# A planned two-branch kernel (S4D convolution and Hedgehog attention): Abs as an operation of its own, new planned durations, new order

## The chip, the cores and the metric

The kernel runs on one core of one Trainium2 chip. The metric is the device time of one execution in microseconds. The engines are TensorE (PE; its weight loads are listed as PEld), VectorE (DVE), ScalarE (ACT), GpSimd (POOL) and SyncE (SP), whose queue issues every transfer of this kernel. L12 is line 12 of the kernel before.

## The reference, cut to what matters

Two branches that do not depend on each other share the output, 576 columns each, for 2048 positions.

```python
# A: S4D. K is made from 576 x 128 modes, then a causal convolution along 2048 positions.
P = exp((A * dt[:, None])[:, :, None] * pos)          # A = -exp(log_A_real) + 1j * A_imag
K = 2.0 * einsum("dn,dnl->dl", C, P).real
y = irfft(rfft(u_t, 2 * L) * rfft(K, 2 * L))[..., :L] + u * D_skip
# B: linear attention, 32 heads of 18, with a learned feature map
q, k, v = split(x @ wqkv)                             # 576 -> 3 x 576
phi_q = concat(softmax(q @ w_phi), softmax(-q @ w_phi))   # phi_k likewise
o = phi_q @ (phi_k.T @ v) / (phi_q @ sum(phi_k) + 1e-6)
b = o @ wo
out = concat(a, b)
```

## The kernel before, in words

Branch B. The feature weights are folded into the weights of k and q (`fold`, L472 to L488): five blocks of wkT, each times w_phi on TensorE, then split on ScalarE and VectorE into a high and a low part, wh and wl. The weights of v (and later of the output) are loaded in thirds and split the same way (`whole`, L503 and L504). Sixteen key tiles of 128 positions follow: the tile of x is loaded, split into xh and xl (L512, L436), and multiplied in three products (`gemm`, 378, 378 and 396 columns wide). Each is three times as many matmuls as its size, since high and low parts are multiplied apart. Then come the two softmaxes (`softmax`, L547 to L559) and a product into kvt, which all sixteen tiles add to. Sixteen query tiles do the same with 2 x 288 columns, turn the features with TensorE (L646), multiply them with kv, divide, turn again (L676) and multiply with the output weights.

Branch A. The Fourier transforms are products with small matrices. `u_first` makes the first step for u (16 blocks). The 36 groups make the convolution kernel K: GpSimd adds phases as whole numbers (`phases`, L853 to L858) in cs[:, 1], a tile of 128 x 1040; `waves` (L868 to L870) turns them into a cosine and a sine on ScalarE, three instructions in one operation of the plan: the absolute value of the phases into cs[:, 0], the sine of the phases, the sine of (pi/2 minus the absolute value). `group` multiplies out the exponents on TensorE (L422, `ps<-sel,mg`), takes Exp on ScalarE (L891), multiplies them on VectorE with the waves (L897 to L902, into cs and E) and sums over the modes on TensorE (`ps<-E,cs`). After each 9 groups `k_first` transforms that quarter. Sixteen products and sixteen last steps follow (`product`, `last`), the products half by half of the columns; each product loads its parts from DRAM and writes back there.

What sets the order. Nothing runs in the order of the text. Each operation is recorded with its engine, a planned duration, and the buffers that it reads and writes (`op`). `run` then plays the kernel through with a clock for each engine, takes again and again the operation that can start first (with ties by a due time), and emits its instructions. A due time is the WANT of the unit (a key tile, a group, a product) minus the LEAD of its step. Some operations have two engines to choose from (`copy` with "any": ScalarE or VectorE; `tt` with two engines: GpSimd or VectorE), and `run` gives them to the engine on which they end first, with LEAN_ACT or LEAN_POOL as a handicap. Where the play has TensorE idle before a new PSUM buffer is written, `emit` puts products of zeros there (L213, fillers), whose result is overwritten, so that TensorE stays busy. The play takes TensorE at half rate for a window when it was little used in the window before. A transfer is played as 625 ns of SP, a start at 1300 ns, a duration by `c_dma`, and LAG until others see it; a change of the shape in which TensorE's array is used (`mode`) costs it extra. Planned durations go into the order alone: the chip does not know them.

The lines that the change touches are the LAG table (L166), the costs in `run` (L319 to L334), `c_dma` (L366), the tables of STAY, LEAN, LEAD and WANT (L372 to L401), the planned cost of `gemm` (L530), `waves` (L864 to L872) and the planned cost of the exponents in `group` (L889).

Of the kernel before, what the change touches and what calls it, by code (L numbers as in the profile page):

```python
# [11 lines left out]
I32 = mybir.dt.int32  # L12
AF = mybir.ActivationFunctionType
# [144 lines left out]
class Plan:  # L158
# [4 lines left out]

    LAG = dict(pe=200.0, dve=135.0, act=150.0, pool=110.0, sp=100.0)  # L166

    def __init__(self):
        self.ops, self.pools, self.free, self.window, self.strict = [], {}, {}, {}, {}
# [46 lines left out]
    def run(self):  # L216
# [48 lines left out]
        while done < n:  # L265
# [50 lines left out]
            self.engine[k] = e  # L316
            self.emit(k, o, e, nf)
            self.start[k] = s
            cost = 625.0 if e == "sp" else o[1] if e == o[0] else o[12][1]  # L319
            if e == "pe":  # L320
                while win < s // WINDOW:
                    warm = used >= (0.375 if warm else 0.7) * WINDOW
                    win, used = win + 1, 0.0
                extra = 50.0 if o[10] == mode else 95.0 + o[10][1] / 1.2
                mode = o[10]
                cost *= 1 if warm else 2
                used += cost * o[7]
                cost += extra if warm else 2 * extra
# [44 lines left out]
LEAD = dict(g1=510.8480, g2=65.9825, g3=1186.0588, g4=-101.5925, k1=55.5339, k2=-7.9693, k3=78.1520, k4=-179.0201, l1=-298.6070, p1=496.9566, p2=-165.1848, p3=26.4674, p4=392.3588, q1=25.7015, q2=-3.5201, q3=-402.9704, q4=-159.0330, q5=-59.1678, q6=-965.4445, u1=1381.3374)  # L373
FILL = 222.0


WANT = dict(
    ident=[-39.703],
    fold=[-3814.5703, -4514.447, 174.1103, 544.6624],
    start=[726.2842],  # L380
    key=[-2909.7917, -0.0799, 220.563, 157.8162, -225.5153, 173.04, -1241.6879, -109.3988, -338.4576, -175.3779,
          -2318.8196, 176.0873, 249.8555, 251.9596, -231.4053, 99.8816],
    kv=[85.5267],
    query=[476.857, 1690.9897, 4431.7125, 751.3041, 2777.2337, 589.8585, 3194.9953, 2789.5574, 367.711, 1380.6418,
          914.5124, 1423.5053, 2499.5972, 1377.3193, 2733.1361, 817.2673],
    u=[-102.8226, -226.0234, -1433.3706, -445.0721, -485.8874, -1597.2828, 880.8324, -734.4783, 728.5016, 739.4667,
          -177.0395, 249.377, -557.77, 773.8434, 166.2647, -5869.6701],
    mags=[-2640.9703],
    sel=[-2760.3264, -489.0097],
    dsk=[46.8315],  # L390
    par=[-3778.6822, 2.4322, 9.7494, 463.2853, 408.4987, 743.2542],
    group=[-219.8582, -466.9395, -327.3681, -1227.057, -1108.9783, -1278.4472, -63.1016, -322.7369, -865.4363, 67.264,
          -45.5422, 473.8194, 485.4349, 462.8623, 544.4259, 128.5531, 59.2296, -27.0576, 750.8126, 602.241, 749.2426,
          752.9731, 692.4676, 603.6052, 928.9227, 702.8443, 689.0661, 1091.0495, 1745.4579, 1177.32, 1030.5714,
          1356.2207, 1245.0883, 1029.2843, 1226.1579, 1186.6316],
    kfirst=[-2069.12, -388.4536, -152.51, 676.399],
    product=[580.2793, 583.4571, 524.945, 1019.1475, 645.2543, 381.769, 375.2706, 687.6813, 2038.1628, 2418.0025,
          2088.0002, 1103.4417, 2475.9162, 1427.038, 1252.1902, 1625.8165],
    last=[326.0515, 549.9183, 360.8347, 614.2391, 1189.7141, 171.5588, 558.2575, -103.0095, 1111.1706, 1441.7724,
          1346.2631, 1230.7698, 2479.1252, 3727.1339, 1655.5831, 3612.5906],  # L400
)  # L401


def body(tc, nc, i, out, ctx):
# [113 lines left out]
    def gemm(x, w, done, ps, o, cs):  # L518

        (xh, xl), (wh, wl) = x, w  # L520

        def f():
            p = o()
            for k in range(4):
                mm(p, xh.t[:, k, :], wh.t[:, k, cs], k == 0, False)
                mm(p, xh.t[:, k, :], wl.t[:, k, cs], False, False)
                mm(p, xl.t[:, k, :], wh.t[:, k, cs], False, False)
            mm(p, xh.t[:, 4, :], wh.t[:, 4, cs], False, False)
            mm(p, xh.t[:, 4, :], wl.t[:, 4, cs], False, True)
        op("pe", 14 * max(110, (cs.stop - cs.start) / 2.4 + 11.5), f, r=[xh, xl, *done], w=[ps], with_=[wh, wl], busy=0.93)  # L530

    def gemm_halves(x, w, done, c0):
        r = []
# [330 lines left out]
    def waves(cs):  # L864
        pl.step("g1")

        def f():
            act.activation(cs.t[:, 0], cs.t[:, 1].bitcast(I32), AF.Abs)  # L868
            act.activation(cs.t[:, 1], cs.t[:, 1].bitcast(I32), AF.Sin, scale=TURN)  # L869
            act.activation(cs.t[:, 0], cs.t[:, 0], AF.Sin, scale=-TURN, bias=hp.t)  # L870
        op("act", 3 * c_act(65 * W) + 370, f, r=[cs, hp], w=[cs], table="sin")
        return cs  # L872

    def group(g, par, cs, ks):
# [7 lines left out]
        def size(k, n):  # L882
            ps = [B("ps", [128, W, 32]) for _ in range(n)]

            def f():
                for h in range(n):
                    hs = slice(64 * h, 64 * h + 64)
                    mm(ps[h].t.rearrange("p x y -> p (x y)"), mg.t[hs, gi, :], sel.t[hs, k:k + 512])
            op("pe", 233, f, r=[mg, sel, cs], w=ps, with_=[E], mode=(64, 128))  # L889
            for p in ps:  # L890
                op("act", c_act(512), lambda p=p: act.activation(p.t, p.t, AF.Exp), r=[p], w=[p], table="exp")  # L891
            return ps
# [186 lines left out]
```

## Time and profile before

| | before |
|---|---|
| time, median of 3 runs | 623.44 us (620.82 to 626.74) |
| the profiled execution, its own time | 622.21 us |
| its span | 620.4 us |
| mean granted clock of TensorE | 0.979 |
| instructions in the profile | 19048 |

The page gives one execution. Its first part is the busy time of each engine, with the share of the span and the number of instructions. A row of a group is line, engine, operation, output from input, shapes and count; then the busy time and the mean length of one; then the engine's idle time ahead of them, and who ended it. A row of a window is its start and end, its length, then busy time and count for each engine (PE, PEld, DVE, ACT, POOL, or for the instructions of one line alone), the granted clock of TensorE, the share of the transfer engines and GB/s. A row of a timeline is start, length, engine, line, operation and count. A row of waits is who waited, for whom, the total, the number of times and the longest.

### The profile page before, as it was taken

To read this page: it belongs to the slowest core of one execution; us is meant where nothing else is said; L and a number is where in the kernel's file an instruction comes from. 1 tells how busy PE (TensorE), PEld (TensorE's weight loads), DVE (VectorE), ACT (ScalarE), POOL (GpSimd) and SP (SyncE) were. 2 spreads that over 40 slices of the span, in tenths; PEclk is the share of its full clock that TensorE was granted. 3 is DMA by queue.
4 is the path that set the end of the run, shared out by engine and by line. 5 is a ranking of instruction groups with operands and counts; after the bars stand their busy time and mean duration, and the time that the engine had idled before them with its cause. 6 is when DMAs were issued, how large, how long until landed. Compare 5 with 4: busy or idle time off the path is not lost.

```text
span 620.4 us, 19048 instructions
## 1 busy us (share of the span) xinstructions
PE 588.6 (95%) x7734; PEld 462.5 (75%) x7737; DVE 557.9 (90%) x1269; ACT 401.1 (65%) x605; POOL 269.1 (43%) x438
## 2 busy tenths in 40 slices
PE   8997999999999987998899999999999999999996
PEld 4687998999998765876666776668778867677775
DVE  3998999999999998999999999999998779987773
ACT  3868749889775399859687988898844322432120
POOL 0465356868451456255275685473301043233000
PEclk9997999999999998997999998999999999999999
DMA  8757110111123665655847668856563787876476
GB/s 230 223 206 234 46 43 23 45 51 50 45 65 99 157 209 203 214 178 151 238 137 237 193 197 227 230 169 211 161 192 88 194 278 220 244 222 220 156 225 195
DMA packets 97789, 104.01 MB, mean 168 GB/s; under 512 B 10534, under 2 KB 84134, under 8 KB 97702
## 3 DMA queue, kind: packets, MB, share of 16 engines
q1 hardware_dynamic: 97702, 102.80, 55.6%
q8 instruction: 61, 1.00, 0.7%
q14 instruction: 26, 0.21, 0.1%
HBM read 63.63 MB, written 39.06 MB: 166 GB/s over the span
## 4 chain that ended last, share of the span: by engine, by line
PE 59%; DVE 21%; ACT 9%; DMA 6%; issue 3%; SPq 1%; DVEq 0%; ACTq 0%
PE ps L422 55%; DVE ac L440 3%; PE ps L646 2%; DVE E L898 2%; DVE cs L897 2%; DVE total L557 2%; DMA dt<-in_ldt_dram 2%; DMA dram<-zi 1%; ACT cs L870 1%; ACT cs L868 1%; DVE E L902 1%; ACT cs L869 1%; DVE E L900 1%; PE ps L213 1%; ACT ps L891 1%
## 5 line engine op out<-in xcount | busy, mean ns | idle before, releaser
L422 PE MATMUL ps<-wh,xl 128*128 128x288 f32 (+2 forms) x448 | 141.5, 316 | 0.6 <-DVE xl L436 0.5
L422 PE MATMUL ps<-wh,xh 128*128 128x378 f32 (+2 forms) x400 | 134.6, 337 | 1.4 <-ACT zi L427 0.6
L422 PE MATMUL ps<-wl,xh 128*128 128x378 f32 (+2 forms) x400 | 129.3, 324 | 0.7 <-DVE wl L488 0.7
L858 POOL TENSOR_TENSOR cs<-cs,pi 128x512 int32<-128x512 int32 (+4 forms) x180 | 115.2, 644 | 10.1
L422 PEld LDWEIGHTS ps<-wh,xh 128*128 128x128 f32 x400 | 76.4, 191 | 14.0 <-issue 4.1
L422 PEld LDWEIGHTS ps<-wh,xl 128*128 128x128 f32 x448 | 85.1, 190 | 1.1 <-DVE xl L436 1.1
L422 PEld LDWEIGHTS ps<-wl,xh 128*128 128x128 f32 x400 | 76.5, 191 | 1.0 <-DVE wl L488 1.0
L891 ACT ACTIVATE ps<-ps 128x512 f32<-128x512 f32 x108 | 56.5, 580 | 9.3 <-PE ps L422 9.0
L436 POOL TENSOR_TENSOR ac<-ac 128x288 f32<-128x288 f32 x55 | 43.3, 808 | 41.8 <-DVE ac L440 32.3
L436 POOL TENSOR_TENSOR xl<-xi,xh 128x512 fp32r<-128x512 f32 x22 | 31.2, 1417 | 64.1 <-PE ps L422 30.1
L213 PE MATMUL ps<-zero 128*32 128x256 bf16 (+11 forms) x270 | 51.5, 327 | 3.2 <-DVE zero L456 1.2
L555 ACT ACTIVATE e<-e 128x1152 f32<-128x1152 f32 x32 | 37.4, 1169 | 22.8 <-DVE e L436 17.9
L440 DVE TENSOR_TENSOR ac<-us,ps 128x288 f32<-128x288 f32 x128 | 48.6, 444 | 1.7 <-issue 0.9
L422 PE MATMUL ps<-E,cs 128*32 128x64 f32 x2304 | 42.7, 224 | 7.2 <-DVE E L900 4.6
L422 PEld LDWEIGHTS ps<-E,cs 128*32 128x32 f32 x2304 | 35.2, 111 | 18.5 <-DVE E L900 7.1
L422 PE MATMUL ps<-wh,xi 128*128 128x288 f32 x160 | 48.9, 308 | 0.0
L512 ACT ACTIVATE xh<-xi 128x640 fp32r<-128x640 f32 x32 | 23.6, 738 | 36.5 <-DMA xi<-in_xT_dram 23.7
L422 PE MATMUL ps<-wl,xi 128*128 128x288 f32 x160 | 46.9, 295 | 0.0
L897 DVE TENSOR_TENSOR cs<-ps,cs 128x1024 f32<-128x1024 f32 x36 | 43.7, 1214 | 3.5 <-ACT ps L891 3.3
L422 PEld LDWEIGHTS ps<-kvb,fT 126*128 126x128 f32 (+1 forms) x320 | 38.2, 189 | 8.5 <-issue 2.1
L213 PEld LDWEIGHTS <-zero 128*128 128x128 bf16 (+6 forms) x273 | 25.9, 103 | 23.8 <-issue 12.1
L898 DVE TENSOR_TENSOR E<-ps,cs 128x1024 f32<-128x1024 f32 x36 | 43.6, 1210 | 0.1
(145 smaller groups left out, 1340.5 us busy)
## 6 DMA issues: line engine op xcount, KB each, us to landing
xi<-in_xT_dram SPq DMA_DIRECT2D x32, 320.0 KB
dram<-zi SPq DMA_DIRECT2D x16, 576.0 KB
dram<-zi SPq DMA_DIRECT2D x32, 288.0 KB
ub<-dram SPq DMA_DIRECT2D x32, 288.0 KB
kb<-dram SPq DMA_DIRECT2D x32, 288.0 KB
dram<-zo SPq DMA_DIRECT2D x32, 288.0 KB
zi<-dram SPq DMA_DIRECT2D x16, 576.0 KB
ub<-in_u_dram SPq DMA_DIRECT2D x16, 288.0 KB
```

What stands on the lines that cost most here:

```text
L213: self.matmul(t[0:cols, 0:n], self.zero.t[0:rows, 0:cols], self.zero.t[0:rows, 0:n])
L422: pe.matmul(o, l, r, start=start, stop=stop, skip_group_check=skip)
L436: op(eng, [c_dve(n) if e == "dve" else c_pool(n) for e in eng], lambda e: (dve if e == "dve" else pool).tensor_tensor(dst(), a(), b(), op= ...
L440: op(eng, c_dve(n) if eng == "dve" else c_pool(n), lambda: e.tensor_tensor(dst(), a(), b(), op=alu), r=r, w=w, lock=eng == "pool" or not a ...
L512: op("act", c_act(640) + 40, lambda: act.activation(xh.t, xi.t, AF.Copy), r=[xi], w=[xh])
L555: op("act", c_act(1152) + 40, lambda: act.activation(e.t, e.t, AF.Exp), r=[e], w=[e], table="exp")
L557: op("dve", 1270, lambda: dve.tensor_reduce(sm.t.rearrange("p h s -> p s h"), e.t, axis=AX.X, op=ALU.add), r=[e], w=[sm])
L646: pe.transpose(tp.t[0:m, j - j0, :], e.t[:, sign, 7 * g:7 * g + GRP[g], :].rearrange("p h f -> p (h f)"), ident.t)
L858: op("pool", c_pool(2 * n * W), lambda n=n, j=j: pool.tensor_tensor(x()[:, :, :, n:2 * n], x()[:, :, :, 0:n], pi.t[:, j:j + 2, gs].bitcast ...
L891: op("act", c_act(512), lambda p=p: act.activation(p.t, p.t, AF.Exp), r=[p], w=[p], table="exp")
L897: op("dve", c_dve(64 * W), lambda: dve.tensor_tensor(F(), both(M.t), F(), op=ALU.mult), r=[M, cs], w=[cs])
L898: op("dve", c_dve(64 * W), lambda: dve.tensor_tensor(E.t[:, :, :, 32:64], both(up.t), cs.t[:, :, :, 0:32], op=ALU.mult), r=[up, cs], w=[E])
```

## The change

`waves` becomes two operations of the plan. The absolute value may run on ScalarE (the same instruction as before) or on VectorE (as the greater of x and -x); the two sines stay one operation on ScalarE. All other edits are planned durations, LAG, and the tables of due times, which were all set anew. What `run` emits therefore differs in order on all five engines, in which engine takes an operation that may choose, and in the number of fillers and of table loads.

```diff
-    LAG = dict(pe=200.0, dve=135.0, act=150.0, pool=110.0, sp=100.0)
+    LAG = dict(pe=200.0, dve=135.0, act=150.0, pool=110.0, sp=700.0)
...
-            cost = 625.0 if e == "sp" else o[1] if e == o[0] else o[12][1]
+            cost = 560.0 if e == "sp" else o[1] if e == o[0] else o[12][1]
...
-                extra = 50.0 if o[10] == mode else 95.0 + o[10][1] / 1.2
+                extra = 20.0 if o[10] == mode else 95.0 + o[10][1] / 1.2
...
-                dma = max(dma, s + 1300.0) + o[1]
-            end[k] = (max(dma, s + 1300.0 + 2.4 * o[1]) if e == "sp" else at[e]) + self.LAG[e]
+                dma = max(dma, s + 1050.0) + o[1]
+            end[k] = (dma if e == "sp" else at[e]) + self.LAG[e]
...
 def c_dma(nbytes, run=4096):
-    return nbytes * (1 if run >= 512 else 2) / 230.0
+    return nbytes / run * max(3.0, 0.57 + 0.0026 * run)
...
-STAY, TURNOVER, NEAR, LEAN_POOL, LEAN_ACT = 39.6166, 43.0853, 13.9405, 412.6640, -488.3109
+STAY, TURNOVER, NEAR, LEAN_POOL, LEAN_ACT = 112.6105, 755.4590, 4.0251, 605.1518, -89.6140
...
-        op("pe", 14 * max(110, (cs.stop - cs.start) / 2.4 + 11.5), f, ...)
+        op("pe", 14 * max(110, (cs.stop - cs.start) / 2.4 + 11.5) + 40 * (cs.stop - cs.start > 288), f, ...)
...
     def waves(cs):
         pl.step("g1")
 
+        x = lambda: cs.t[:, 1].bitcast(I32)
+
         def f():
-            act.activation(cs.t[:, 0], cs.t[:, 1].bitcast(I32), AF.Abs)
-            act.activation(cs.t[:, 1], cs.t[:, 1].bitcast(I32), AF.Sin, scale=TURN)
+            act.activation(cs.t[:, 1], x(), AF.Sin, scale=TURN)
             act.activation(cs.t[:, 0], cs.t[:, 0], AF.Sin, scale=-TURN, bias=hp.t)
-        op("act", 3 * c_act(65 * W) + 370, f, r=[cs, hp], w=[cs], table="sin")
+        op(("act", "dve"), (c_act(65 * W), c_dve(65 * W)), lambda e: act.activation(cs.t[:, 0], x(), AF.Abs) if e == "act" else
+           dve.scalar_tensor_tensor(cs.t[:, 0], x(), -1.0, x(), op0=ALU.mult, op1=ALU.max), r=[cs], w=[cs])
+        op("act", 2 * c_act(65 * W) + 330, f, r=[cs, hp], w=[cs], table="sin")
         return cs
...
-            op("pe", 233, f, r=[mg, sel, cs], w=ps, with_=[E], mode=(64, 128))
+            op("pe", 280, f, r=[mg, sel, cs], w=ps, with_=[E], mode=(64, 128))
...
```

The tables LEAD (20 numbers) and WANT (137 numbers) are new throughout. `LEAN_ACT` is added to VectorE's end time where ScalarE or VectorE may take an operation, so a negative value draws work to VectorE: it goes from -488 to -90. `LEAN_POOL` does the same against GpSimd: it goes from 413 to 605. `TURNOVER`, which delays an operation that needs another activation table, goes from 43 to 755.

More of the change, by code (lines that the diff above doesn't have):

```diff
@@ L374 @@
+LEAD = dict(g1=717.3351, g2=116.1613, g3=870.2954, g4=316.3489, k1=45.5644, k2=-7.6480, k3=404.7042, k4=-244.5601, l1=-164.5009, p1=154.5135, p2=-288.8656, p3=276.2322, p4=267.8751, q1=-27.4168, q2=-127.6535, q3=-397.9354, q4=-327.2321, q5=-145.0983, q6=-1071.3161, u1=1521.8018)
 FILL = 222.0
 WANT = dict(
[L378 to L398, printed above, removed]
@@ L399 @@
-    last=[326.0515, 549.9183, 360.8347, 614.2391, 1189.7141, 171.5588, 558.2575, -103.0095, 1111.1706, 1441.7724,
-          1346.2631, 1230.7698, 2479.1252, 3727.1339, 1655.5831, 3612.5906],
+    ident=[-140.4884],
+    fold=[-6573.2593, -4263.9457, 236.3216, 481.1985],
+    start=[938.4289],
+    key=[-3994.6221, 194.3063, -347.7404, 145.2637, 185.889, -2489.373, -532.9443, -394.3828, 122.7302, 242.6108,
+          102.6971, -1701.6086, -390.9243, -2208.1311, -68.4662, 170.5283],
+    kv=[165.939],
@@ new lines @@
+    query=[4192.9302, 327.2233, 933.9411, 3593.8802, 469.6671, 1449.5377, 2404.4648, 2702.5713, 2610.3179, 2760.4261,
+          944.9876, 486.0401, 1374.6561, 4088.7994, 2262.1284, 1106.6026],
+    u=[-37.306, 398.6079, -245.04, -69.9386, 523.7635, -396.0958, 733.4493, 1186.397, -509.4818, 824.7191, 830.8135,
+          -3308.0724, 1176.0487, -1343.8654, -427.1056, -671.9534],
+    mags=[-3917.6976],
+    sel=[-2135.7029, -3130.1049],
+    dsk=[457.6569],
+    par=[-4018.2262, -63.0204, 95.8465, 209.1831, 854.5163, 941.7482],
@@ new lines @@
+    group=[-1283.8625, -2005.4707, -531.4461, -1705.4247, -774.1315, -802.936, -292.3883, -1589.5841, -895.0975,
+          377.9042, 12.4366, 235.5928, 524.2006, 575.3788, 282.8035, 657.7546, 415.9221, 146.5749, 1014.2309,
+          1236.5945, 713.9374, 1529.0259, 1206.4456, 1274.1266, 847.9414, 744.8986, 700.6586, 1802.8903, 2267.2791,
+          2025.9291, 2408.2812, 2087.062, 2784.6067, 4067.2411, 1957.6071, 2529.9992],
+    kfirst=[-2641.9488, -206.815, 298.6813, 689.0919],
+    product=[119.154, 1013.8548, 794.6474, 684.7031, 982.7207, 458.4306, 149.54, -161.639, 1615.9638, 1423.6008,
+          2432.7582, 1670.783, 1563.7102, 1440.234, 1910.5064, 2444.3737],
@@ L401 @@
+    last=[773.0148, 1207.0956, 737.2483, 1015.6201, 1217.0438, 649.601, 1375.5222, 2035.5654, 2640.4165, 2742.6446,
+          2449.247, 2347.5194, 2597.0062, 1800.3776, 3584.9657, 2777.1016],
 )
@@ L529, in f @@
             mm(p, xh.t[:, 4, :], wl.t[:, 4, cs], False, True)
-        op("pe", 14 * max(110, (cs.stop - cs.start) / 2.4 + 11.5), f, r=[xh, xl, *done], w=[ps], with_=[wh, wl], busy=0.93)
+        op("pe", 14 * max(110, (cs.stop - cs.start) / 2.4 + 11.5) + 40 * (cs.stop - cs.start > 288), f, r=[xh, xl, *done], w=[ps], with_=[wh, wl], busy=0.93)
     def gemm_halves(x, w, done, c0):
```

1 line of the change is left out of this document (removed).

## The prediction

> **What bounds the kernel now.** I read the page's engine totals first, then cut the span at two points that both programs have: the last product that the key tiles add to kvt, and the last value that VectorE writes into E for the last of the 36 groups.
>
> ```profile
> PE 588.6 (95%) x7734; PEld 462.5 (75%) x7737; DVE 557.9 (90%) x1269; ACT 401.1 (65%) x605; POOL 269.1 (43%) x438
> 208.14 0.20 PE L422 MATMUL ps<-e,v 128*19 128x36 f32 x1
> 471.01 0.68 DVE L902 SCALAR_TENSOR_TENSOR E<-ps,cs 128x512 f32<-128x512 f32 x1
> core 0: us, PE busy (x) PEld busy (x) DVE busy (x) ACT busy (x) POOL busy (x), PEclk, DMA share, GB/s
> 0.00:208.30 208.30, 200.05 (x2649) 172.53 (x2653) 189.50 (x402) 150.09 (x206) 106.10 (x171) 0.98 0.37 106
> 208.30:471.70 263.40, 246.57 (x3610) 181.44 (x3603) 252.11 (x565) 211.05 (x317) 133.15 (x230) 0.97 0.65 194
> 471.70:620.40 148.70, 141.98 (x1491) 108.53 (x1490) 116.26 (x304) 39.92 (x83) 29.81 (x37) 0.99 0.68 207
> 0.00:208.30 208.30, 20.85 (x98) 9.99 (x98) 0.98 0.37 106
> 208.30:471.70 263.40, 20.15 (x122) 10.68 (x124) 0.97 0.65 194
> 471.70:620.40 148.70, 10.55 (x50) 5.27 (x51) 0.99 0.68 207
> 52.13 0.34 PE L422 MATMUL ps<-wh,xl 128*128 128x378 f32 x1
> 52.30 0.33 PE L422 MATMUL ps<-wh,xh 128*128 128x378 f32 x1
> ```
>
> The first window rows give every engine, the second three the filler products of L213 alone. Two engines look full. But TensorE's share holds 51.6 us (20.85 + 20.15 + 10.55) of fillers, which multiply zeros while the plan expects nothing ready, and its busy time counts a product for 0.34 us although the next one starts 0.17 us later (last two rows), so a short gap behind a product stays invisible. VectorE's 252.1 of 263.4 us in the middle stage (96%) is work that must be done. So I read: up to 471.7 us VectorE sets the pace (441.6 of 471.7 us, 93.6%), with TensorE close behind; after it TensorE does (142.0 of 148.7 against VectorE's 116.3). The Trainium skill ("Perfetto Trace Analysis", section "Identifying the Most-Contended Engine") says the same of such totals: occupancy is a fair measure for VectorE, while matmul busy time is not one for TensorE. By that rule VectorE would be called the bound; the 0.34 and 0.17 us agree with it.
>
> **The change part by part.** The new planned costs (transfers, TensorE's change of shape, the 40 ns on wide gemms, 280 for the exponents) issue nothing; they and the new WANT and LEAD tables act through the order and through the engine that the plan chooses. So I compared the two built instruction lists. Real TensorE work and transfers are the same in number. What differs: 35 fillers fewer (273 to 238), 20 activation table loads fewer (58 to 38), VectorE 82 instructions fewer (1271 to 1189), ScalarE 50 more, GpSimd 12 more. The prices:
>
> ```profile
> L436 DVE TENSOR_TENSOR e<-e,small 128x1152 f32<-128x1152 f32 x14 | 19.5, 1395 | 0.1
> L427 DVE COPY fT<-ps 126x512 f32<-126x512 f32 x19 | 12.6, 682 | 1.0 <-PE ps L646 0.8
> L427 DVE COPY zi<-ps 128x288 f32<-128x288 f32 x75 | 30.0, 445 | 1.2 <-PE ps L422 1.0
> L427 DVE COPY ks<-ps 128x256 f32<-128x256 f32 x27 | 11.2, 415 | 0.3 <-PE ps L422 0.3
> L427 DVE COPY v<-ps 128x396 f32<-128x396 f32 x9 | 5.0, 554 | 0.0
> L427 DVE COPY v<-ps 128x180 f32<-128x180 f32 x13 | 4.3, 339 | 1.8 <-PE ps L422 1.7
> L436 DVE TENSOR_TENSOR ac<-ac 128x288 f32<-128x288 f32 x9 | 6.2, 690 | 0.0
> L436 DVE TENSOR_TENSOR xl<-xi,xh 128x512 fp32r<-128x512 f32 x10 | 8.4, 838 | 0.0
> L897 DVE TENSOR_TENSOR cs<-ps,cs 128x1024 f32<-128x1024 f32 x36 | 43.7, 1214 | 3.5 <-ACT ps L891 3.3
> L836 DVE TENSOR_SCALAR fx<-pi 128x384 f32<-128x384 f32 x6 | 2.1, 350 | 0.0
> L753 DVE SCALAR_TENSOR_TENSOR ac<-ac,ks 128x640 f32<-128x640 f32 x1 | 0.8, 818 | 0.0
> L868 ACT ACTIVATE cs<-cs 128x1040 f32<-128x1040 int32 x36 | 38.5, 1069 | 0.4 <-POOL cs L858 0.4
> L869 ACT ACT_TABLE_LOAD x26 | 33.4, 1283 | 0.5
> L427 ACT ACTIVATE zi<-ps 128x288 f32<-128x288 f32 x53 | 18.9, 410 | 19.9 <-PE ps L422 19.0 <-ACT zi L427 0.8
> L427 ACT ACTIVATE fT<-ps 126x512 f32<-126x512 f32 x13 | 7.5, 601 | 3.4 <-PE ps L646 3.4
> L436 POOL TENSOR_TENSOR ac<-ac 128x288 f32<-128x288 f32 x55 | 43.3, 808 | 41.8 <-DVE ac L440 32.3 <-PE ps L646 9.4
> L436 POOL TENSOR_TENSOR e<-e,small 128x1152 f32<-128x1152 f32 x2 | 4.4, 2200 | 4.6 <-DVE small L559 4.5
> L436 POOL TENSOR_TENSOR xl<-xi,xh 128x512 fp32r<-128x512 f32 x22 | 31.2, 1417 | 64.1 <-PE ps L422 30.1 <-ACT xh L512 28.1 <-DVE E L902 5.5
> ```
>
> *Abs by itself.* Of 36 only 5 move to VectorE, 3 before and 2 after the first milestone; the other 31 stay on ScalarE, as instructions that other work may now be put between. On VectorE no row shows it. By element the nearest rows give 350 / 384 x 1040 = 0.95 us (L836), 818 / 640 x 1040 = 1.33 us (L753) and 1.23 us (L897, of nearly its size). I take 1.2; 5 x 1.2 = 6.0 us onto VectorE, 4.8 to 6.7 between the ends. ScalarE gives up 5 x 1.07 = 5.3 us.
>
> *VectorE up to the second milestone.* Gone from its queue: 6 multiplications of 1152 (8.4 us), 10 copies of fT at 0.682 (6.8), 15 of zi at 0.445 (6.7), 11 of yo and 3 of us at the same 0.445 (6.2), 9 of ks (3.7), 5 + 5 of v (4.5), 3 sums of ac (2.1), 5 small copies of fT at about 0.41 (2.0): 40.4 us. New on it: 5 Abs (6.0), 4 splits of xl (3.4), 3 copies of zo (1.3), and 9.8 us of instructions that stood behind the milestone before, nearly all the softmax and division of one query tile: 20.5 us. Net 40.4 - 20.5 = 19.9 us less; by busy time rather than length it is a little less, since neighbours overlap (the 75 zi copies are busy 30.0 us, 0.40 each against 0.445), so I use 18. If VectorE alone set the pace at its 93.6%, that is 18 / 0.936 = 19.2 us. But TensorE's work up to there does not shrink, and it comes next: I count three quarters, 14 us, with 0 and 19 as ends.
>
> *Where that work goes.* On ScalarE 75 copies more (22 of fT, 16 of zi, 10 each of ks, v and yo, 5 of ot, 5 of us, 3 fewer of zo) cost about 33 us; 20 table loads (25.7) and 5 Abs (5.3) pay for them: plus 2 us in all, and 6 less up to the second milestone, where ScalarE was at 80%. Cost at nothing, because the loads that go hide it. GpSimd gets 9 sums of ac (7.3), 6 multiplications of 1152 (13.2) and one small one, and loses 4 splits of xl (5.7): some 16 us more on an engine at 43%, cost at nothing. Its cover is that the key tile's multiplication may end 0.8 us later (2.2 for 1.4): who waits for it is the product into kvt, and behind that on TensorE's queue the next gemm. If none of the 6 is covered, that is 4.8 us.
>
> *Start.*
>
> ```profile
> 15.32 0.34 SPq L476 DMA_DIRECT2D e<-in_wkT_dram  x1
> 24.71 0.44 PE L422 MATMUL ps<-wh,xh 128*128 128x378 f32 x1 [0.35 <-ACT wh L487]
> 28.35 0.43 SPq L463 DMA_DIRECT2D zi<-in_wv_dram  x1
> 39.96 0.34 PE L422 MATMUL ps<-wh,xh 128*128 128x396 f32 x1
> 10.81 2.75 PE L422 MATMUL ps<-fT,e 126*128 126x126 f32 x20 [1.83 <-DMA e<-in_wkT_dram]
> ```
>
> SP's queue now begins with phi and all five blocks of wkT; the fifth stood at place 16, behind wv, parameters, xi and magnitudes, and was issued at 15.3 us. The folds can follow each other, and the first gemm, at 24.7 us until now, can start up to 8 us earlier. But the third kind of gemm needs the last third of wv, issued at 28.4 us and used from 40.0; it still stands in the queue behind the first two writes of gd, which wait for the magnitudes (places 13 to 14 instead of 15 to 17). And only 4 fillers in place of 22 run ahead of the folds, so the folds may run at the low clock: 50 products at 2.75 / 20 us are 6.9 us, at half rate as much again. Minus 8 to plus 7; I take minus 3, nearer to the wv load, which barely moves, than to the first gemm.
>
> *The queue of transfers elsewhere.* SP issues the same 390 in another order. The chain that ended last (below) gives all transfers 6%, 37 us; another order can gain or lose a few us of that, with nothing in this profile to say which. I cost it at nothing.
>
> *Last stage.* TensorE's real work there is the same to within 1%. Of its 50 fillers (10.55 us) 18 are left: 32 x 0.21 = 6.8 us. A filler that goes leaves either work or a wait; with one query tile fewer to finish and VectorE at 78% I count half, 3.4 us, ends 0 and 6.8.
>
> *Sum.* 14 + 3 + 3.4 = 20.4 us off a span of 620.4 gives 600.0, and off the profiled execution (622.2; it lies 1.2 below the median of 623.4) 601.8. Off the median: 603.
>
> **The rivals.**
>
> *TensorE is the bound already.* For it: 95% busy, 59% of the chain that ended last. Then VectorE's relief is worth nothing and only fillers count: 35 x 0.19 (51.55 / 270) = 6.7, with 3 from the start 9.7: 613.7. Against it: its busy time double-counts (0.34 for 0.17), and weight loads wait 7.5 us for E from VectorE.
>
> ```profile
> PE 59%; DVE 21%; ACT 9%; DMA 6%; issue 3%; SPq 1%; DVEq 0%; ACTq 0%
> PEld ps L422 <- DVE E L900: 7.5, 9, 1.6
> ACT zi L427 <- PE ps L422: 19.0, 16, 2.8
> 40.00:80.00 40.00, 36.83 (x371) 33.70 (x370) 36.05 (x83) 32.94 (x43) 16.27 (x27) 0.91 0.44 133
> ```
>
> *The moved copies wait on ScalarE.* They stand in order behind Abs, Sin, Sin (over 1.05 us each) and their table loads (1.28), and hold one of 8 PSUM buffers. If each of the 75 frees its buffer 0.27 us later on TensorE's path, 20 us are gone: 623. For it: ScalarE at 80% in the middle. Against it: there ScalarE waits for TensorE rather than the other way round (its zi copies 19.0 us).
>
> *The clock, and so slower.* The granted clock falls to 0.91 in the slice 40 to 80 us, which is about 7.2 us at half rate ((1 - 0.91) x 40 x 2) and costs half of that, 3.6 us. Fillers are what keeps TensorE busy between products, and 35 go. From 8 more such stretches than now the time is 603 + 28.8 = 632. The Trainium skill ("TensorE: Matmul & The Clock Gate", section "What's actually happening") has the rule: half rate is the default, and an idle window of about 3.4 us brings it back. By that rule fewer fillers alone do nothing, long gaps do. Against the rival: from 80 to 120 us not one filler ran (the row is L213's alone) and the clock was 1.00, on real work only; a faster VectorE makes that denser.
>
> ```profile
> 80.00:120.00 40.00, 0.00 (x0) 0.00 (x0) 1.00 0.13 36
> ```
>
> **How the numbers follow.** Forecast (VectorE's relief, start, fillers: 603): 0.60. TensorE bound (614): 0.17. Copies wait on ScalarE (623): 0.12. Clock (632): 0.11. About 1% is what a measurement of this kernel tells from no change, 617.2 to 629.7; so faster 0.77, same 0.12, slower 0.11. All low ends together would be 623 - 19 - 8 - 7 = 589, which is not to be had at once; from 591 up to 622, which takes in the second case and most of the third's lower half, some 2 in 10 are left out.
>
> **What would show it.** Right: VectorE's busy time near 520 us (557.9 - 37 for the whole list), with a share under 93% up to the last E; that milestone near 455 instead of 471.7; 38 table loads; the first gemm before 22 us. Wrong: VectorE at 520 but TensorE's fillers and gaps as long as before (TensorE bound); PE waiting for ScalarE's copies in the list of waits; PEclk under 1 in more than five of the 40 us slices.

## The result, and the profile after

The changed kernel takes 627.67 us (median of 20 runs, 624.04 to 630.99) against 620.71 us (618.42 to 626.74) of the kernel before: ratio 1.0103, 95% interval 1.0079 to 1.0127, so 6.4 us slower where 603 us had been forecast. The profiled execution has a span of 624.4 us, 4.0 more than the 620.4 before.

The lines of the page and of the windows that answer to those of the kernel before: the engine totals; the three stages, cut at the same two points (the last product into kvt, now at 203.0 us; the last write of E, now at 481.2 us); and the fillers of L213 alone in the same three stages (PE, then PEld).

```profile
PE 577.7 (93%) x7702; PEld 459.8 (74%) x7702; DVE 530.0 (85%) x1187; ACT 396.7 (64%) x655; POOL 283.1 (45%) x450
0.00:203.00 203.00, 188.92 (x2682) 165.13 (x2683) 182.12 (x385) 145.81 (x218) 115.03 (x185) 0.97 0.40 114
203.00:481.20 278.20, 254.12 (x3574) 193.03 (x3573) 248.36 (x543) 203.28 (x333) 130.80 (x220) 0.97 0.53 161
481.20:624.40 143.20, 134.70 (x1450) 101.67 (x1448) 99.52 (x260) 47.61 (x105) 37.26 (x46) 1.00 0.82 252
0.00:203.00 203.00, 11.86 (x62) 5.96 (x63) 0.97 0.40 114
203.00:481.20 278.20, 26.69 (x159) 15.24 (x159) 0.97 0.53 161
481.20:624.40 143.20, 4.10 (x18) 1.73 (x18) 1.00 0.82 252
```

Three numbers per stage say where the time went. TensorE's real work is its busy time less the fillers, and its idle time is the length less the busy time:

| stage | length, before to after | real work | fillers | idle |
|---|---|---|---|---|
| keys | 208.3 to 203.0 | 179.2 to 177.1 | 20.9 to 11.9 | 8.3 to 14.1 |
| groups | 263.4 to 278.2 | 226.4 to 227.4 | 20.2 to 26.7 | 16.8 to 24.1 |
| end | 148.7 to 143.2 | 131.4 to 130.6 | 10.6 to 4.1 | 6.7 to 8.5 |

TensorE's work is the same in each stage to within 2.1 us; what changed is how long it waits or runs fillers. The first stage gained 5.3 us, the last 5.5, and the middle lost 14.8, of which 13.8 are fillers and idle time. Nearly all of that (12.6 us) lies in one stretch of 40 us. Here it is in the kernel before (all engines, then L213 alone):

```profile
440.00:480.00 40.00, 39.67 (x535) 32.63 (x536) 37.07 (x80) 21.07 (x36) 5.61 (x6) 1.00 0.54 156
440.00:480.00 40.00, 0.50 (x2) 0.19 (x2) 1.00 0.54 156
```

And in the kernel after:

```profile
440.00:480.00 40.00, 36.13 (x479) 29.65 (x478) 33.25 (x65) 27.94 (x41) 9.86 (x14) 0.96 0.08 26
440.00:480.00 40.00, 9.57 (x63) 6.42 (x63) 0.96 0.08 26
```

TensorE had 39.2 us of real work there and has 26.6 now, and the transfers' share fell from 0.54 to 0.08. SP's queue shows why nothing came: after the load of xi at 447.1 it stands for 35 us at the store of one query tile's ot, in order.

```profile
439.82 0.37 SPq L464 DMA_DIRECT2D xi<-in_xT_dram  x1
440.31 0.45 SPq L690 DMA_DIRECT2D out_dram<-ot  x1
447.10 0.37 SPq L464 DMA_DIRECT2D xi<-in_xT_dram  x1
481.96 0.35 SPq L690 DMA_DIRECT2D out_dram<-ot  x1
```

In the kernel before, seven last steps of the first half (each a load of zi, a product with w3, two copies and two stores) ran in this stretch or just ahead of it, from 427 to 467 us. In the new order these seven stand behind the writes of k_first, so the last groups run with little beside them, each a chain of Exp, four products on VectorE and 64 matmuls on one buffer of E.

A second place stands out at 215 to 241 us. Here are SP's queue, then TensorE, then a window over all engines, all of the kernel after.

```profile
215.20 6.24 SPq L622 DMA_DIRECT2D kvb<-ot  x7
221.55 0.40 SPq L728 DMA_DIRECT2D dram<-zi  x1
222.00 0.80 SPq L622 DMA_DIRECT2D kvb<-ot  x1
222.91 0.49 SPq L728 DMA_DIRECT2D dram<-zi  x1
223.45 4.96 SPq L622 DMA_DIRECT2D kvb<-ot  x6
228.51 0.41 SPq L717 DMA_DIRECT2D ub<-in_u_dram  x1
```

```profile
231.60 2.38 PE L423 MATMUL ps<-ub,w 64*128 64x288 f32 x8 [3.96 <-DMA ub<-in_u_dram]
```

```profile
231.00:241.00 10.00, 9.40 (x37) 7.23 (x38) 5.79 (x13) 7.33 (x10) 2.25 (x1) 0.50 0.84 258
```

Fourteen transfers of 5.3 to 6.7 KB each hold the queue for 0.8 us apiece or a little more; the load of u behind them is issued at 228.5, TensorE waits 3.96 us for it, and the ten us after that run at a granted clock of 0.50. The kernel before has the same fourteen transfers, from 212.7 to 226.8 us, but there two loads of u stand among them:

```profile
215.49 0.41 SPq L716 DMA_DIRECT2D ub<-in_u_dram  x1
219.07 0.41 SPq L716 DMA_DIRECT2D ub<-in_u_dram  x1
```

The Trainium skill ("TensorE: Matmul & The Clock Gate", section "What's actually happening") says that an idle window of about 3.4 us brings half rate; the 3.96 us of waiting in the kernel after, and the 0.50 behind it, agree.

### The profile page after: what moved, and what is told of

Read it like the earlier page. It is cut to its first block, busy times and chain, and to the rows that moved or that the text cites. A ratio compares the mean times of both kernels' runs of the same rounds, so it can differ in the third digit from the quotient of the medians.

```text
span 624.4 us, 19005 instructions
## 1 busy us (share of the span) xinstructions
PE 577.7 (93%) x7702; PEld 459.8 (74%) x7702; DVE 530.0 (85%) x1187; ACT 396.7 (64%) x655; POOL 283.1 (45%) x450
## 4 chain that ended last, share of the span: by engine, by line
PE 52%; DVE 26%; DMA 10%; ACT 5%; issue 3%; POOL 2%; SPq 1%; DVEq 0%; POOLq 0%
PE ps L423 47%; DMA zi<-dram 3%; DVE cs L901 3%; DVE E L902 3%; DVE e L437 2%; PE ps L213 2%; DVE E L906 2%; DVE E L904 2%; PE ps L647 2%; DMA zi<-in_wv_dram 1%; DVE small L558 1%; DVE ac L441 1%; PE ps L677 1%; DVE zi L428 1%; DVE small L548 1%
## 5 line engine op out<-in xcount | busy, mean ns | idle before, releaser
L859 POOL TENSOR_TENSOR cs<-cs,pi 128x32 int32<-128x32 int32 (+4 forms) x180 | 113.6, 632 | 11.5
L437 POOL TENSOR_TENSOR ac<-ac 128x288 f32<-128x288 f32 x64 | 50.4, 811 | 58.0 <-DVE ac L441 43.2
L213 PE MATMUL ps<-zero 128*32 128x256 bf16 (+10 forms) x238 | 42.6, 316 | 1.3 <-DVE zero L457 1.2
L872 ACT ACTIVATE cs<-cs,hp 128x1040 f32<-128x1040 f32 x36 | 41.4, 1149 | 0.0
L423 PE MATMUL ps<-kvb,fT 126*128 126x133 f32 (+1 forms) x320 | 40.4, 277 | 0.0
L854 POOL MEMSET cs<- 128x16 f32 x36 | 4.6, 129 | 78.6 <-PE ps L423 68.0
```

The costliest lines, as they stand in the source:

```text
L213: self.matmul(t[0:cols, 0:n], self.zero.t[0:rows, 0:cols], self.zero.t[0:rows, 0:n])
L423: pe.matmul(o, l, r, start=start, stop=stop, skip_group_check=skip)
L437: op(eng, [c_dve(n) if e == "dve" else c_pool(n) for e in eng], lambda e: (dve if e == "dve" else pool).tensor_tensor(dst(), a(), b(), op= ...
L859: op("pool", c_pool(2 * n * W), lambda n=n, j=j: pool.tensor_tensor(x()[:, :, :, n:2 * n], x()[:, :, :, 0:n], pi.t[:, j:j + 2, gs].bitcast ...
```

## The experiments

Three theories. **T1** has two halves: TensorE's own work is the pace, so that VectorE's relief is worth nothing, and the waits of the new order are the loss. **T2**, the prediction's: VectorE sets the pace, its relief is worth some 14 us, so the order must cost more than that. **T3**: the copies moved to ScalarE are waited for. The kernels that change the order emit the plan's recorded list (operation, engine, fillers ahead of it) with the lines of the diff changed; all else is the kernel named.

**The two halves of the change, each alone.** The engine choices of after in the order of before, and the reverse.

```diff
-order = [(k, engine_before[k], fillers[k]) for k in order_before]
+order = [(k, engine_after[k] if k in flexible else engine_before[k], fillers[k]) for k in order_before]
```

> The order of the kernel before, instruction by instruction, and its Abs on ScalarE; only the engine of 287 flexible operations is that of the kernel after (the copies and casts that went from VectorE to ScalarE or GpSimd and back). T1, the pace is TensorE's own work plus the waits that the order leaves, and the relief of VectorE is worth nothing: within 3 us of the kernel before (ratio 0.995 to 1.005), VectorE's busy time some 25 us lower. T2, the prediction's, VectorE sets the pace up to the last write of E: 10 to 15 us faster (ratio about 0.98), that milestone near 460. T3, the moved copies wait on ScalarE: 3 to 8 us slower, with TensorE waiting for ScalarE's copies more than before.

> The order of the kernel after, with the engine choices of the kernel before for the same 287 operations and every Abs on ScalarE. T1: the order alone brings the loss, so within 3 us of the kernel after (ratio to the kernel before 1.005 to 1.015). T2: the new order costs about 24 us by itself and the lighter VectorE hides most of it, so 12 to 20 us slower than the kernel after (ratio 1.03 to 1.04). T3: the order is good or neutral and ScalarE's copies are what lost, so about as fast as the kernel before or faster (ratio 0.98 to 1.00).

Measured: engines alone 1.0374 (1.0337 to 1.041), order alone 1.0841 (1.0796 to 1.0886). Both are slower than the two together (1.0103), and slower than any theory had expected: the first by 23 us, where T3 had 3 to 8, the second 46 us behind the kernel after, where T2 had 12 to 20. VectorE's list of waits, of the kernel before and of the run with after's engines:

```profile
DVE cs L897 <- ACT ps L891: 3.3, 5, 1.6
```

```profile
DVE cs L897 <- ACT ps L891: 20.9, 15, 4.2
```

TensorE's list, of the kernel after and of the run with before's engines in its order:

```profile
PE ps L423 <- DVE E L904: 6.7, 8, 2.1
PE ps L423 <- DVE E L906: 3.3, 13, 0.3
```

```profile
PE ps L423 <- DVE E L904: 17.2, 13, 2.9
PE ps L423 <- DVE E L906: 6.3, 15, 1.5
```

In an order that was not made for them, the copies on ScalarE stand ahead of an Exp that VectorE waits for: this wait grows by 17.6 us. With VectorE's old load, E comes late in the new order: these two rows grow by 13.5 us, which leaves most of the 46 us unexplained. So order and engine choice are one plan and their values do not add: neither half can be priced by its busy time.

**The load of u behind the kvb transfers.** A line is one issue in SP's queue, in order; the edit puts the two loads back among the transfers.

```diff
 kvb, kvb
+load ub (block 1)
 kvb, kvb
+load ub (block 4)
 kvb x10, two writes of zi
-load ub (block 1)
 load e (wo), load mg, mg
-load ub (block 4)
```

> The kernel after with two loads moved in SP's queue: two of the blocks of u (the loads of ub that stood behind the fourteen kvb transfers at 215 to 228 us) are issued before or between them; nothing else. T1: TensorE's wait of 4 us at 227.6 to 231.6 us goes, and with it the half-rate stretch behind it (10.2 us of the span at half rate, so up to 5 more): 3 to 9 us faster than the kernel after (ratio to the kernel before 0.996 to 1.005). T2: VectorE sets the pace and TensorE's wait was slack: within 2 us of the kernel after (ratio about 1.010).

Measured: 1.0073 (1.0045 to 1.0101), some 1.9 us less than the kernel after, which the intervals do not tell from nothing. Both kernels run the same products on TensorE in the same order, so each product's start can be set beside its twin (us: kernel after, this run, difference):

```
231.60  225.01   -6.59  ps<-ub,w
240.69  230.47  -10.22  ps<-wh,xl
241.36  234.84   -6.52  ps<-ub,w
309.25  305.67   -3.58  ps<-sel,mg
427.35  425.49   -1.86  ps<-zi,w
575.57  575.00   -0.56  ps<-ub,ff
```

The wait of 3.96 us goes and 10 us are gained for a moment, as T1 had it. Then the next load of u is late instead (the row below), and of the rest only 0.6 us is left some 330 us further on. The total is what T2 had forecast, within 2 us of the kernel after.

```profile
PE ps L423 <- DMA ub<-in_u_dram: 3.8, 1, 3.8
```

**The last steps back among the last groups.** First with each load only 4 to 5 us ahead of its product:

```diff
 groups 28, 30, 35, 32
-20, 19 and 18 fillers ahead of three of their products
+load zi, product with w3, two copies, two stores   (seven times)
 k_first, quarter 3
-the same seven steps
```

> The kernel after with seven last steps of the first half (load, product with w3, two copies, two stores each) moved from behind the k_first writes (500 to 545 us) into the stretch of the last groups (425 to 470 us), where the kernel before had them; the 57 fillers of three steps there are taken out. T1: these steps fill TensorE's waits at 440 to 482 us and take DMA traffic out of 520 to 560 us, where the DMA queues are full: 6 to 13 us faster than the kernel after (ratio to the kernel before 0.99 to 1.00). T2: the last groups are paced by VectorE's products, so the moved copies and products change nothing before the last write of E and only the end gets shorter by their 10 us of TensorE work at most: within 4 us of the kernel after.

Measured: 1.0346 (1.0304 to 1.0387), 15 us worse than the kernel after. TensorE's waits between 430 and 488 us:

```profile
PE ps L423 <- DMA zi<-dram: 9.6, 2, 6.0
PE ps L423 <- DVE E L904: 4.8, 2, 2.9
```

The edit itself made this wait: products stood in TensorE's queue ahead of E,cs while their zi was still on its way. So this run tells nothing of the theories, only that filling a hole needs the data there. So the same steps again, with the loads issued as soon as a buffer of zi comes free and the products at the holes:

> The kernel after, with the seven last steps of the first half in the stretch of the last groups as in the run before, but each load of zi issued at least 8 us ahead of its product (as soon as a buffer comes free, in the 35 us in which SP's queue stands idle), the products put where TensorE ran fillers (430, 440, 453, 461 and 466 us), the copies on the engine that is idle there; the 57 fillers of three steps are taken out. T1, the order left TensorE uncovered at 440 to 482 us: 6 to 13 us faster than the kernel after (ratio to the kernel before 0.990 to 1.001), fillers and idle time of TensorE at 440 to 480 us 13 us less, and the DMA share over 0.3 there. T2, the groups are paced by VectorE's products and the moved steps only come on top: the last write of E moves 5 us or more later, the end stays within 3 us of the kernel after.

Measured: 1.0053 (1.0022 to 1.0085), some 3.1 us less than the kernel after. All engines in the stretch, then L213:

```profile
440.00:480.00 40.00, 33.73 (x417) 25.65 (x420) 30.17 (x59) 28.35 (x43) 10.65 (x16) 0.87 0.41 121
440.00:480.00 40.00, 1.17 (x5) 0.48 (x5) 0.87 0.41 121
```

TensorE's real work there rises from 26.6 to 32.6 us, but with most fillers gone the granted clock falls to 0.87, and idle time grows from 3.9 to 6.3 us: part of the gain is given back. Fillers and idle time together are 6.0 us less there, where T1 had 13, and the whole is 3.1 us faster, where T1 had 6 to 13. The last write of E comes 5.8 us later, at 487.0, as T2 had it, but the stage behind it is 8.9 us shorter, which T2 had not.

> The kernel after with both moves of the two earlier runs together: the two loads of ub taken out from behind the kvb transfers, and the seven last steps in the stretch of the last groups, each load issued early. Of the 57 fillers taken out there eleven come back (3 and 8), so that TensorE's clock is held up. If the two waits are what the order of the kernel after lost and the two moves add up: 1.9 and 3.1 us, so 5 us faster than the kernel after, and 2 to 4 more where the clock stays up (ratio to the kernel before 0.996 to 1.002). If each gain is given back at the next wait: no faster than the better of the two alone (ratio 1.005 to 1.008).

Measured: 0.9989 (0.9960 to 1.0017): 7.1 us less than the kernel after, level with the kernel before. In the stretch, all engines and L213:

```profile
440.00:480.00 40.00, 34.82 (x462) 26.05 (x462) 32.54 (x66) 29.28 (x47) 9.76 (x14) 0.96 0.44 129
440.00:480.00 40.00, 3.05 (x17) 1.49 (x17) 0.96 0.44 129
```

So the two places together are worth the whole difference that was measured, 6.4 us. Whether they add exactly (1.9 + 3.1 against 7.1) the intervals do not tell, and eleven fillers came back as well; with them the granted clock in the stretch is 0.96 again.

**What sets the pace: work added to one engine.** Per group, on VectorE a reduction that nobody reads, on TensorE three fillers more, on ScalarE three small copies.

```diff
+    for _ in range(NG):      # VectorE, behind the group's last write of E
+        op("dve", 600, lambda: dve.tensor_reduce(junk.t[:, 0:1], sel.t[:, 0:512].bitcast(F32), axis=AX.X, op=ALU.max), r=[sel], w=[junk])
...
+            act.activation(junk.t, sel.t[:, 0:32].bitcast(F32), AF.Copy)   # ScalarE, three times behind the third Exp
```

> The kernel before in its own order, with one reduction over a constant tile more on VectorE behind the last write of E of each of the 36 groups (some 0.55 us each, 20 us in all; nothing reads it). T2, VectorE sets the pace to the last write of E: 12 to 20 us slower (ratio 1.02 to 1.033). T1, TensorE's work sets the pace: 0 to 6 us slower (ratio below 1.01).

> The kernel before in its own order, with three more fillers on TensorE ahead of the first sel,mg product of each of the 36 groups (108 of about 0.22 us, 24 us in all). T1, TensorE's work sets the pace: 18 to 25 us slower (ratio 1.03 to 1.04). T2, VectorE sets it and TensorE waits for it: 0 to 12 us slower (ratio below 1.02).

> The kernel before in its own order, with three copies of 128x32 more on ScalarE behind the third Exp of each of the 36 groups (108 of some 0.2 us, 20 us or more in all; nothing reads them). If ScalarE has the slack that the prediction gave it (64% busy): 0 to 5 us slower (ratio below 1.008). T3, work on ScalarE is waited for: 10 us or more slower (ratio above 1.016).

> The kernel after in its own order, with the same 36 reductions more on VectorE (20 us in all). T1: 0 to 6 us slower than the kernel after (ratio to the kernel before 1.010 to 1.02). T2, with the relief the pace has gone to TensorE: also below 6 us. Should VectorE still set the pace in spite of its 28 us less: 12 to 20 us slower than the kernel after (ratio 1.03 to 1.042).

> The kernel after in its own order, with three more fillers ahead of the first sel,mg product of each of the 36 groups (108 of about 0.27 us, 29 us in all, as in the kernel before, where they cost 13 us). If TensorE has become the pace in place of VectorE: 18 to 28 us slower than the kernel after (ratio to the kernel before 1.04 to 1.055). If it waits for others as before: 8 to 15 us slower than the kernel after (ratio 1.023 to 1.035).

> The kernel after in its own order, with the same 108 copies more on ScalarE. If ScalarE has slack: 0 to 5 us slower than the kernel after (ratio to the kernel before 1.010 to 1.018). T3, the pace of the kernel after lies with ScalarE's copies and waves: 12 to 22 us slower than the kernel after (ratio 1.03 to 1.046), more than the same work costs the kernel before.

One row gives the length of the added instruction on VectorE, one that on ScalarE (ns, least, median and most):

```profile
L1060 DVE TENSOR_REDUCE junk<-sel x36: 664/678/682, 85.9 to 491.1; 128x1 f32<-128x512 f32 x36
```

```profile
L1062 ACT ACTIVATE junk<-sel x108: 221/230/250, 78.4 to 468.4; 128x32 f32<-128x32 f32 x108
```

| added | to the kernel before | to the kernel after (ratio, less 1.0103) |
|---|---|---|
| VectorE, 36 x 0.678 = 24.4 us | 1.0328 (1.0273 to 1.0384), +20.4 us | 1.0243 (1.0184 to 1.0302), +8.7 us |
| TensorE, 108 fillers, busy on L213 from 51.5 to 80.5 = 29.0 us (kernel after: 28.1) | 1.0211 (1.0154 to 1.0268), +13.1 us | 1.0180 (1.0131 to 1.0230), +4.8 us |
| ScalarE, 108 x 0.230 = 24.8 us | 1.0002 (0.9971 to 1.0032), +0.1 us | 1.0159 (1.0100 to 1.0219), +3.5 us |

The kernel before pays nearly in full for work on VectorE, about half for fillers on TensorE, and nothing on ScalarE. The first half of T1 falls: added work on VectorE cost 20.4 us, where T1 had 0 to 6. T2 holds for VectorE (12 to 20 us), but TensorE is close behind, with 13.1 us where T2 had 0 to 12. The kernel after pays less for VectorE and TensorE, and less for TensorE than either forecast had (8 us or more); its 8.7 us for VectorE lie between the two forecasts, up to 6 and from 12. That there more of the time is waiting, into which added work fits, would explain it, but no run shows it. What ScalarE's copies cost it, 3.5 us, is not clear of nothing.

**The other direction: work taken off VectorE,** with the order and the engines kept.

```diff
-        ... dve.tensor_reduce(sm.t..., e.t, axis=AX.X, op=ALU.add)
+        ... dve.tensor_reduce(sm.t..., e.t[:, :, :, 0:6], axis=AX.X, op=ALU.add)
```

```diff
-    F = lambda: cs.t[:, :, :, 33:65]
+    F = lambda: cs.t[:, :, 0:8, 33:65]      # and M cut to the same 8 rows
```

> The kernel before in its own order and with its own engines; the sums of the softmax (32 reductions of 1.34 us on VectorE) read 6 of the 18 values of each head, which leaves out two thirds of that sum: some 0.85 us less each, 27 us in all, about 22 of it ahead of the last write of E. Nothing is moved to another engine. T2, a relief of VectorE is worth what the prediction gave it (0.7 us for each us): 15 to 19 us faster (ratio 0.97 to 0.976). If the order is such that only added work counts and less work is not taken up by TensorE: 0 to 5 us faster (ratio 0.992 to 1.0).

> The kernel after in its own order, with the same 27 us less on VectorE (the sums of the softmax read 6 of the 18 values of each head, so two thirds of that sum are left out). If the kernel after is no longer paced by VectorE: 0 to 4 us faster than the kernel after (ratio to the kernel before 1.004 to 1.010), less than the 6 us that it brought the kernel before. If VectorE still paces it through its latency in the chains: 5 to 8 us faster (ratio 0.997 to 1.002).

> The kernel before in its own order and with its own engines; the first product of each of the 36 groups on VectorE (cs times M, 1.2 us) covers 8 of the 16 rows, which leaves out the other half of that product: some 0.55 us less each, 20 us in all, at the place where the run with added work put its 24 us, and this time on the chain from Exp to E,cs itself. If the small answer to less work was due to its place in the softmax: 12 to 20 us faster (ratio 0.968 to 0.98). If less work on VectorE is taken up only in part wherever it lies: 3 to 8 us faster (ratio 0.987 to 0.995).

> The kernel after with the same 20 us less in the first product of its groups. If its groups run alone at the end (440 to 482 us), where the chain from Exp to E,cs is bare, some 3 us of this are sure (six groups, 0.55 us each), and of the rest a quarter, as for the softmax: 5 to 9 us faster than the kernel after (ratio to the kernel before 0.996 to 1.002). If VectorE's chain paces all of its groups: 12 to 20 us faster (ratio 0.978 to 0.991).

The shortened instructions, first in the softmax (1.342 us before), then in the groups (1.214 us before):

```profile
L557 DVE TENSOR_REDUCE small<-e x16: 535/542/555, 50.4 to 199.1; 128x64 f32<-128x384 f32 x16
```

```profile
L897 DVE TENSOR_TENSOR cs<-ps,cs x36: 615/681/693, 77.1 to 456.5; 128x512 f32<-128x512 f32 x36
```

| taken off VectorE | from the kernel before | from the kernel after (ratio, less 1.0103) |
|---|---|---|
| softmax, 32 x 0.80 = 25.6 us | 0.9902 (0.9864 to 0.9939), -6.1 us | 0.9990 (0.9961 to 1.0020), -7.0 us |
| groups, 36 x 0.533 = 19.2 us | 0.9851 (0.9819 to 0.9883), -9.3 us | 0.9995 (0.9968 to 1.0022), -6.7 us |

A microsecond off VectorE is worth 0.24 us in the softmax and 0.48 in the groups of the kernel before, where a microsecond on it cost 0.84. The place matters by a factor of two, but both stay well under the price of added work. In the kernel before, T2 had expected 15 to 19 us in the softmax and 12 to 20 in the groups; the two reliefs of the kernel after fall in the ranges 5 to 8 and 5 to 9 us that had been named for them. A likely reason is the fixed order: TensorE's next product stands behind others that wait for engines which were not relieved. No run tests this.

**Parts of the change alone, planned anew.** Abs alone with old durations and due times; and Abs with the new durations, but with the old due times. The second run also has the old values of the next table (LEAN, TURNOVER and the rest), which its expectation does not say:

```diff
-STAY, TURNOVER, NEAR, LEAN_POOL, LEAN_ACT = 112.6105, 755.4590, 4.0251, 605.1518, -89.6140
+STAY, TURNOVER, NEAR, LEAN_POOL, LEAN_ACT = 39.6166, 43.0853, 13.9405, 412.6640, -488.3109
-LEAD = dict(g1=717.3351, ...); WANT = dict(ident=[-140.4884], ...)
+LEAD = dict(g1=510.8480, ...); WANT = dict(ident=[-39.703], ...)
```

> The kernel before with one part of the change alone: Abs as an operation of its own on ScalarE or VectorE, with the old durations and due times; the planner makes a new order from them. If a part of the change is worth its busy time: within 4 us of the kernel before (ratio 0.994 to 1.006), since at most some ten Abs change their engine. If every new order brings waits of its own, of the size that is in question here, because the due times fit one plan only: 5 to 30 us slower (ratio 1.008 to 1.05).

> The kernel after without its new due times and leads: Abs of its own and the new planned durations, but the old due times. If the new durations describe the chip better and that is what an order lives on: within 6 us of the kernel before or faster (ratio below 1.01). If due times and durations belong together: 10 to 40 us slower than the kernel before (ratio 1.016 to 1.065), slower than the kernel after.

Measured: 1.0835 (1.0771 to 1.0899) and 1.1058 (1.1001 to 1.1114), beyond what had been expected of either. In both, the old handicap (LEAN_ACT at -488) goes with 16 Abs on VectorE, where the kernel after has 5; the row is of the first:

```profile
L873 DVE SCALAR_TENSOR_TENSOR cs<-cs x16: 1220/1234/3297, 42.0 to 492.8; 128x1040 f32<-128x1040 int32 x16
```

At the price of added work that is 16 x 1.234 x 0.84, some 17 us of the 52 lost (an estimate). The other 35 come with the new order. It seems that due times fit one plan, and that a plan of some 3000 operations turns over when a few of them change; which of the old values does it, these two runs do not tell apart. Against a spread of that size the terms of the forecast, 3 to 14 us, are small.

## Why the prediction was wrong

The side was wrong, and two steps failed.

*"I count three quarters, 14 us".* The reading behind it held in part: VectorE was the engine on which more work counts most (20.4 us for 24.4 added). But the price of more is not the price of less. At 0.24 to 0.48 for a microsecond, the 18 us counted are worth 4 to 9; and up to the last E VectorE's busy time fell by 11.1 us only (441.6 to 430.5), worth 3 to 5. The ends of the term, 0 and 19, took that in; the choice within them did not.

*"Another order can gain or lose a few us ... I cost it at nothing."* This step decided the sign. With the relief at 3 to 9, the start at 3 and the last stage at 3.4, the forecast's own sum would be 9 to 15 us off 620.7 (the forecast started from 623.4, the median of three runs; that of twenty is 620.7), so 605 to 611; the kernel takes 620.7 x 1.0103 = 627.1. By this estimate the new order lost 16 to 22 us. It is a rough one, since it adds terms that the two halves of the change showed not to add. The two places found are worth 7.1 of them; that is shown. The other 9 to 15 would lie in waits that were not tried one by one (one is 4.4 us at 303 to 308 us, where TensorE runs fillers and idles until a group's E is written); they stay open. What could have been seen ahead of the result, in the instruction list: the last steps of the first half had moved behind k_first on TensorE, and the u loads behind the kvb transfers on SP. The prediction compared numbers of instructions, not which work stands beside which. For SP the Trainium skill ("Perfetto Trace Analysis", section "What "DMA-bound" means") names the issuing queue, where it is solid with transfers, as a bound of its own; in the 13 us from 215.2 to 228.4 SP's queue is that, and TensorE's 3.96 us behind it agree.

Point by point, the rest. *Abs*: 5 on VectorE at 1.210 us, forecast 1.2:

```profile
L874 DVE SCALAR_TENSOR_TENSOR cs<-cs 128x1040 f32<-128x1040 int32 x5 | 6.1, 1210 | 1.2 <-POOL cs L859 1.2
```

- *VectorE's busy time* fell by 27.9 us, not 37, to 530.0; its share up to the last E is 430.5 / 481.2 = 89%, as forecast, but for a reason that had not been meant: the way to that milestone, forecast near 455, got longer, from 471.7 to 481.2.
- *Table loads*: 38, as forecast.
- *Copies on ScalarE at nothing*: right as a load (24.8 us added cost 0.1), and in the kernel after TensorE waits 6.0 us for them in its list, against 3.7 before; the run with after's engines in the old order shows that it is their place in the queue that could cost, 23 us there, and the new order avoids that.
- *GpSimd*: 14.0 us more where 16 had been counted; whether that costs anything was not tried apart.
- *Start*, -3 with ends -8 and 7: the first gemm starts at 16.2 us instead of 24.7, and the load of the last third of wv, which was to barely move, is issued at 24.5 instead of 28.4. The first stage is 5.3 shorter; how much of that is VectorE's relief is not shown.
- *Last stage*, -3.4 with ends 0 and 6.8: 5.5, in range.

*The rivals.* TensorE as the bound: not alone, by the added work. Copies waiting on ScalarE: no, by the work added there. The clock is the one rival on the right side. Its sign fired, with seven slices under 1 instead of five. In the two profiled executions the mean granted clock is 0.977 against 0.979, worth 0.002 x 624 = 1.2 us by the prediction's price. But that execution of the kernel before had one of its lower clocks: over the 89 runs of that kernel beside the experiments the mean is 0.987, over the 20 of the kernel after 0.980, and by the same price that is 0.007 x 624 = 4.4 us. It does not act alone: the run with the last steps early has 0.975 and is faster than the kernel after, and the run with both moves has 0.981 and is level with the kernel before. At 231 us the low clock follows a wait; how much of it elsewhere is cause and how much consequence is not shown.

## What to carry to other kernels

In a kernel whose order is planned to fill every queue, measure what a microsecond more and a microsecond less on an engine is worth before counting a relief: here 0.84 and 0.24 to 0.48. When the order is new, list for each stretch which work stands beside which and what stands ahead of each load in the issuing queue; equal instruction counts say nothing of it. A stretch in which the transfers' share falls to 0.08 and fillers come up is where the order lost its cover, and here it could be mended only with loads that were issued early enough.

## What the runs showed of the hardware that was not expected

A short instruction of VectorE can count as busy while it seems to wait for GpSimd. One of 208 ns by the median took 2.24 us, next to one of GpSimd that ended with it. So it was with all nine instructions of this line that overran by more than 0.15 us: each ended 0.07 us behind one of GpSimd. VectorE's row, then GpSimd's, of the kernel after:

```profile
235.75 2.24 DVE L805 TENSOR_SCALAR dt<-ax 128x96 f32<-128x96 f32 x1
```

```profile
235.67 2.25 POOL L505 TENSOR_TENSOR wl<-e,wh 128x960 fp32r<-128x960 f32 x1 [4.86 <-ACT wh L504]
```

Instructions of VectorE that took over 0.15 us more than the median of their form add up to some 14 us in the kernel before and some 16 in the kernel after, so a share of 96% in the prediction may have held a few per cent of waiting. And the issue of a transfer on SP does not grow with its bytes: it took 0.8 us for the 5.3 to 6.7 KB of a kvb transfer, and 0.41 us for 288 KB of u.
